# Moving eight of 128 key columns per half tile from VectorE to TensorE in a decode attention kernel

## The chip, the cores and the metric

The kernel runs on one core of a Trainium2 chip. The metric is device time in microseconds (us); lower is better. The profile is one execution taken by the hardware profiler, and its span is a little shorter than the time of a run (657.3 against 658.6 us in the profiled execution of the kernel before).

## The reference, cut to what matters

A decode step for two sequences: normalize `x`, one query for each of 32 heads, attention over a cache of 8192 keys and values a head, output projection, residual, and a small gated FFN.

```python
B, Sq, D = 2, 1, 512
Hq, Hkv, Sk, Dh = 32, 32, 8192, 128
...
scores = jnp.einsum("bhqd,bhkd->bhqk", q, k) * (Dh ** -0.5)
p = _softmax(scores, axis=-1)
o = jnp.einsum("bhqk,bhkd->bhqd", p, v)
```

K and V in bf16 are 2 x 32 x 8192 x 128 x 2 bytes = 134.2 MB each. With the weights the kernel reads 281 MB, each byte once.

## The kernel before: what the argument touches

The 64 pairs of sequence and head are taken in tiles of four (one `o` each), 16 tiles in all: 15 passes of a loop and a tail. A tile of K or of V is 8.39 MB and holds two half tiles, on each partition 128 columns (keys) of 128 values. There is **one buffer for K and one for V**, so a load can be issued only when the last reader of the tile before is done.

The scores of a half tile are shared out. VectorE takes the first `JC` columns: one multiply by q, four adds that halve the width, one reduce. TensorE takes the last `NG` groups of 8: it transposes them, ScalarE copies the transposes out of PSUM, TensorE multiplies them by q.

```python
GT = 8
NG = 4
JC = J - NG * GT          # J = 128 columns, so 96 are VectorE's
...
def k_mult(p, pr):        # VectorE
    return nc.vector.tensor_tensor(
        out=pr[:, 0:JC, :], in0=tile(K, p)[:, 0:JC, :],
        in1=q_c[:, Q2:QW].unsqueeze(1).broadcast_to([128, JC, Dh]), op=ALU.mult)
...
for g in range(NG):       # TensorE, for each half tile
    if g >= 2:
        wait(a2p, ev[g - 2])             # ScalarE has emptied this PSUM bank
    for k in range(GT // 2):
        ... nc.tensor.transpose(Tp[g % 2][...], k_t[:, j:j + 2, :] ...)
    if g >= 1:
        score(g - 1)
score(NG - 1)
```

SyncE issues the loads, all on one queue: K of the next tile when both multiplies (`d2s`) and the transposes (`kf`) are done, V when the last PV matmul is done.

```python
sp.wait((d2s, 2 * o - 1), tokp("kf", p))
if o < NI:
    load(K, A_k_cache, o, k_sem[0])
    sp.wait(tokp("pv", p))
    load(V, A_v_cache, o, v_sem)
```

The softmax here doesn't subtract the row's maximum and nothing guards it: scores larger than these inputs give would overflow.

## Time and profile before

| | before |
|---|---|
| time, median of 3 runs | 658.75 us (658.38 to 660.93) |
| busy: VectorE, TensorE, ScalarE | 467.8, 337.1, 271.2 us |
| DMA queue in use | 99.2% of the span |
| one pass of the loop | 38.70 us |
| V issued ahead of K's landing | 4.3 us |
| K issued ahead of V's landing | 6.1 us |

The last two rows: each is the time that a load, once issued, stands in the queue behind the load before it. I call it the **lead** of that load. While a lead lasts, a tile is still under way. One wait list, SyncE's own in the kernel before (columns: who waited for whom, total us, times, longest):

```profile
SPq L182 <- PE O L418: 303.0, 15, 20.8
SPq L32 <- PE S L378: 236.2, 15, 29.0
SPq L182 <- DVEq L602: 36.3, 15, 3.4
```

V (first line) waits for TensorE's PV matmuls. For K, SyncE waits for the transposes and then, 2.4 us a pass, for VectorE's multiplies: VectorE released K.

### The profile page before, as it was taken

The numbers are of one execution on the slowest core, as the hardware profiler recorded it, in microseconds if no ns is written. First come the engines' busy times: TensorE is split into PE (matmuls) and PEld (weight loads), VectorE is DVE, ScalarE is ACT, GpSimd is POOL, SyncE is SP. The second block draws the span as 40 slices with busy tenths as digits, with TensorE's granted clock in tenths as the row PEclk, the third lists the DMA queues.
The fourth block names the chain that finished last, engine by engine and source line by source line (L and its number), as shares of the span: only waits on it lengthen the run. The fifth ranks groups of instructions, "written<-read, shape, count | busy, mean of one in ns | idle before, by whom it ended". The sixth has DMA issues, their size and how long they took to land.

```text
span 657.3 us, 7744 instructions
## 1 busy us (share of the span) xinstructions
PE 337.1 (51%) x3097; PEld 207.1 (32%) x3097; DVE 467.8 (71%) x275; ACT 271.2 (41%) x687; POOL 95.3 (15%) x96
## 2 busy tenths in 40 slices
PE   2563644646354464534547364454736445473676
PEld 0250431515133151413316141231604224150444
DVE  1188594967949496794949769494985949589881
ACT  1352452625345172524527243352624336262460
POOL 4000011030300203030030303003030210303000
PEclk9955656555565655756565575656556565655566
DMA  9999999999999999999999999999999999999997
GB/s 415 403 428 440 431 423 431 439 439 423 423 447 439 419 427 439 447 439 415 435 435 447 431 419 427 447 447 427 415 435 447 439 431 415 439 447 410 427 421 312
DMA packets 6324, 281.16 MB, mean 428 GB/s; under 512 B 710, under 2 KB 812, under 8 KB 1324
## 3 DMA queue, kind: packets, MB, share of 16 engines
q1 hardware_dynamic: 6308, 281.05, 99.2%
q8 instruction: 5, 0.08, 0.0%
q14 instruction: 3, 0.02, 0.0%
q10 hardware_dynamic: 8, 0.00, 0.0%
HBM read 281.05 MB, written 0.00 MB: 428 GB/s over the span
## 4 chain that ended last, share of the span: by engine, by line
DMA 65%; DVE 32%; PE 2%; issue 1%; ACT 0%; SPq 0%; DVEq 0%; ACTq 0%
DMA K<-in_A_k_cache_dram 59%; DVE X L552 15%; DVE prod L552 15%; DMA K<-in_B_W_down_dram 5%; DVE prod L561 1%; DVE X L561 1%; PE T L395 0%; PE O L418 0%; DVE scores L566 0%; PE Ob L431 0%; ACT e L506 0%; PE O L816 0%; ACT kT L578 0%; SPq L708 0%; PE S L378 0%
## 5 line engine op out<-in xcount | busy, mean ns | idle before, releaser
L418 PE MATMUL O<-V,e 128*16 128x512 bf16 x1024 | 114.7, 612 | 187.6 <-ACT e L506 113.0
L552 DVE TENSOR_TENSOR X<-K,q_c 128x12288 bf16<-128x12288 bf16 x15 | 98.4, 6558 | 141.8 <-DMA K<-in_A_k_cache_dram 141.8
L578 ACT ACTIVATE kT<-T 128x1024 bf16<-128x1024 bf16 x128 | 126.9, 1022 | 151.9 <-PE T L395 148.6
L395 PE MATMUL T<-ident_f,K 128*128 128x128 f32 x512 | 126.0, 410 | 65.3 <-DVEq L598 60.8
L506 ACT ACTIVATE e<-scores 32x96 bf16<-32x96 f32 x128 | 52.9, 414 | 182.1 <-DVEq L609 178.4
L561 DVE TENSOR_TENSOR prod<-prod 128x6144 bf16<-128x6144 bf16 (+1 forms) x68 | 112.7, 1658 | 4.0
L552 DVE TENSOR_TENSOR prod<-K,q_c 128x12288 bf16<-128x12288 bf16 x17 | 111.4, 6553 | 2.9 <-DMA K<-in_A_k_cache_dram 2.1
L395 PEld LDWEIGHTS T<-ident_f,K 128*128 128x128 f32 x512 | 91.5, 211 | 67.4 <-DVEq L598 62.8
L418 PEld LDWEIGHTS O<-V,e 128*16 128x16 bf16 x1024 | 28.6, 117 | 260.6 <-ACT e L506 140.6
L561 DVE TENSOR_TENSOR X<-X 128x6144 bf16<-128x6144 bf16 (+3 forms) x60 | 99.5, 1658 | 3.8
L378 PE MATMUL S<-q_c,kT 128*128 128x8 bf16 x1024 | 48.7, 171 | 35.1 <-ACT kT L578 34.9
L533 POOL MEMSET O_l<- 128x32 bf16 x13 | 1.7, 131 | 422.0 <-DVEq L615 422.0
L378 PEld LDWEIGHTS S<-q_c,kT 128*128 128x128 bf16 x1024 | 42.0, 107 | 63.5 <-ACT kT L578 61.7
L538 POOL COPY rsel<-rows 128x112 bf16<-128x112 bf16 x14 | 44.1, 3151 | 41.2 <-DVEq L615 40.4
L431 PE MATMUL Ob<-sel,os_sb 128*128 128x4 f32 x136 | 30.9, 350 | 11.0 <-ACT os_sb L581 11.0
L431 PEld LDWEIGHTS Ob<-sel,os_sb 128*128 128x128 f32 x136 | 29.4, 319 | 12.9 <-ACT os_sb L581 12.8
L506 ACT ACTIVATE e<-S 32x32 bf16<-32x32 f32 x128 | 29.7, 232 | 2.4 <-PE S L378 0.9
L506 ACT ACTIVATION_READ_ACCUMULATOR e<-scores 32x1 f32 x128 | 29.1, 227 | 0.0
L506 ACT ACTIVATION_READ_ACCUMULATOR e<-S 32x1 f32 x128 | 25.6, 200 | 1.5
L540 POOL TENSOR_TENSOR O_l<-O_cur,mask 128x32 bf16<-128x32 bf16 x14 | 25.0, 1785 | 0.0
L549 POOL COPY q_c<-q_all 128x144 bf16<-128x144 bf16 x16 | 16.2, 1010 | 45.3 <-PE O L418 32.3
L578 ACT ACT_TABLE_LOAD x15 | 19.2, 1283 | 0.3
(106 smaller groups left out, 142.2 us busy)
## 6 DMA issues: line engine op xcount, KB each, us to landing
K<-in_A_k_cache_dram SPq DMA_DIRECT2D x2, 4096.0 KB, 20.8
V<-in_A_wq_dram SPq DMA_DIRECT2D x1, 4096.0 KB, 12.3
V<-in_A_v_cache_dram SPq DMA_DIRECT2D x1, 4096.0 KB, 22.8
X<-in_A_wo_dram SPq DMA_DIRECT2D x1, 3584.0 KB, 16.4
V<-in_A_v_cache_dram SPq DMA_DIRECT2D x1, 3072.0 KB, 29.7
K<-in_B_W_up_dram SPq DMA_DIRECT2D x1, 1376.0 KB, 28.8
K<-in_B_W_gate_dram SPq DMA_DIRECT2D x1, 1376.0 KB, 32.4
V<-in_A_v_cache_dram SPq DMA_DIRECT2D x1, 1024.0 KB, 31.7
```

Source lines behind the costliest of these rows:

```text
L378: i = nc.tensor.matmul(Sp[p % 2][:, A * jj:A * jj + 2 * A], lhsT=kv_[:, k, r, :], rhs=q_c[:, 2 * A * r:2 * A * r + 2 * A], start=(r == 0), ...
L395: i = nc.tensor.transpose(Tp[g % 2][:, k * 128:(k + 1) * 128], k_t[:, j:j + 2, :].rearrange("p j d -> p (j d)").bitcast(F32), ident_f[:])
L418: i = nc.tensor.matmul(Op[0][c:c + 16, :], lhsT=e_t[q][:, j // VJ, :], rhs=v_t[:, j:j + VJ, :].rearrange("p j d -> p (j d)"), start=(q == ...
L431: i = nc.tensor.matmul(Ob[:, 0:A], lhsT=os_sb[:, jj * Dh:(jj + 1) * Dh], rhs=sel[:, A * jj:A * jj + A], start=(jj == 0), stop=(jj == VJ - 1))
L506: i = nc.scalar.activation(out=e_t[q][h, j0 // VJ:j1 // VJ, :].rearrange("p g (j a) -> p g j a", a=A)[:, :, :, a], in_=src(h, a), func=ACT ...
L533: pool.run(e.memset(o_window(o - 1)[0], 0.0))
L538: e.tensor_copy(out=rsel[:, :, o % B, :], in_=bass.AP(x.tensor, x.offset, [list(x.ap[0]), [DR - OS, A], [1, DR]]))
L540: e.tensor_tensor(out=w, in0=O_cur[:].unsqueeze(2).broadcast_to([128, A, NM]), in1=mask[:, off // 4:off // 4 + OS // 4 * (A - 1) + 1:OS // ...
L549: nc.gpsimd.tensor_copy(out=q_c[:], in_=q_all[:, o]).then_inc(g2d, 1)
L552: return nc.vector.tensor_tensor(out=pr[:, 0:JC, :], in0=tile(K, p)[:, 0:JC, :], in1=q_c[:, Q2:QW].unsqueeze(1).broadcast_to([128, JC, Dh] ...
L561: run(nc.vector.tensor_tensor(out=pr[:, 0:JC, 0:w], in0=pr[:, 0:JC, 0:w], in1=pr[:, 0:JC, w:2 * w], op=ALU.add))
L578: to_pe(nc.scalar.activation(out=kT[gg % 2][:], in_=Tp[gg % 2][:].bitcast(BF16), func=ACT.Copy))
```

## The change

The intent: VectorE is the busiest compute engine and its multiplies stand in the chain that ended last, so give eight of its 96 columns to TensorE. One number changes; the rest of the diff follows from it, as ScalarE's counter reaches other values.

```diff
-    NG = 4
+    NG = 5
...
-                EV = 13
+                EV = 15
...
-                    k_part(body, 0, (1, 2, 3, 4), ((k2p, 1),))
-                    k_part(body, 1, (5, 6, 7, 8), ())
-                    collect(body, 9)
-                    pv(body, 0, ((JC, J, ((v_sem, 16), (a2p, 10))), (0, JC, ((a2p, 12),))))
+                    k_part(body, 0, range(1, 6), ((k2p, 1),))
+                    k_part(body, 1, range(6, 11), ())
+                    collect(body, 11)
+                    pv(body, 0, ((JC, J, ((v_sem, 16), (a2p, 12))), (0, JC, ((a2p, 14),))))
...   (the tail's counts likewise)
```

More of the change, by code (lines that the diff above doesn't have):

```diff
@@ L469, in program @@
                 t_ob_loop = (pe.sem, tail.at["ob"])
-                k_part(tail, P0, (2, 3, 4, 5), ((k2p, 1),))
-                k_part(tail, P1, (7, 8, 9, 10), ((k2p, 2),))
-                nc.tensor.wait_ge(a2p, 12)
+                k_part(tail, P0, range(2, 7), ((k2p, 1),))
+                k_part(tail, P1, range(8, 13), ((k2p, 2),))
+                nc.tensor.wait_ge(a2p, 14)
                 nc.tensor.wait_ge(sem_wo, 16)
@@ L478, in program @@
                 tail.mark("op", i)
-                pv(tail, P0, ((JC, J, ((v_sem, 16),)), (0, JC, ((a2p, 13),))))
-                nc.tensor.wait_ge(a2p, 14)
+                pv(tail, P0, ((JC, J, ((v_sem, 16),)), (0, JC, ((a2p, 15),))))
+                nc.tensor.wait_ge(a2p, 16)
                 for c in range(DC):
@@ L484, in program @@
                         start=False, stop=False, skip_group_check=True)
-                pv(tail, P1, ((V_LAST, J, ((sem_vl[0], 16), (a2p, 15))), (0, V_LAST, ((a2p, 15), (sem_vl[1], 16)))),
+                pv(tail, P1, ((V_LAST, J, ((sem_vl[0], 16), (a2p, 17))), (0, V_LAST, ((a2p, 17), (sem_vl[1], 16)))),
                    lambda: tail.mark("z", z_sum(Sp[0])))
@@ L722, in program @@
                 sums()
-                collect(tail, 16)
+                collect(tail, 18)
                 dve.wait(tok("ob", NI))
```

## The prediction

> **What bounds the kernel now.** I began with the page's header, slices and queues.
>
> ```profile
> PE 337.1 (51%) x3097; PEld 207.1 (32%) x3097; DVE 467.8 (71%) x275; ACT 271.2 (41%) x687; POOL 95.3 (15%) x96
> ...
> DMA  9999999999999999999999999999999999999997
> ...
> q1 hardware_dynamic: 6308, 281.05, 99.2%
> ```
>
> No compute engine is above 71% of the span, while the 16 DMA engines are nine tenths busy or more in every slice but the last, and one queue's packets fill 99.2% of their time. The kernel reads a cache once: 281.05 MB at the page's 428 GB/s is 656.7 us, the whole span of 657.3 us. The change alters no byte.
>
> The chain that ended last looks less simple: DMA 65%, DVE 32%, with the two multiplies of line 552 (K times q, 96 columns each) at 15% each. In order of time, one loop pass reads:
>
> ```profile
> 422.46 6.56 DVE X L552
> 429.02 6.48 DVE prod L552
> 435.58 25.46 DMA K<-in_A_k_cache_dram
> 461.03 0.04 DVEq L598
> ```
>
> So K lands, VectorE multiplies its two half tiles for 13.1 us, the buffer is free, the next K is issued and lands 25.46 us later: a loop of 38.7 us. The reader is to ask whether those 25.46 us are transfer or queueing. SyncE's timeline gives the issue times, and TensorE's shows when V landed:
>
> ```profile
> 417.97 0.33 SPq L182 DMA_DIRECT2D V<-in_A_v_cache_dram  x1
> 435.58 0.33 SPq L182 DMA_DIRECT2D K<-in_A_k_cache_dram  x1
> 456.69 0.33 SPq L182 DMA_DIRECT2D V<-in_A_v_cache_dram  x1
> ...
> 441.72 1.03 PE L418 MATMUL O<-V,e 128*16 128x512 bf16 x8 [4.50 <-DMA V<-in_A_v_cache_dram]
> ```
>
> V, issued at 417.97, landed at about 441.7; K, issued at 435.58, had **6.1 us** to stand in the queue behind it. K's remaining 461.03 - 441.7 = 19.3 us are its transfer: 8.39 MB in 19.3 us is 434 GB/s. The next V was issued at 456.69, **4.3 us** before K landed at 461.03. There is thus always a tile under way when the next is issued. A pass moves 16.78 MB, and 16.78 MB / 38.70 us = 433.5 GB/s, the same rate. The busy time by stretches confirms it (columns: stretch, length, then busy time of PE, PEld, DVE, ACT, POOL, the clock, DMA share, GB/s):
>
> ```profile
> 447.00:452.00 5.00, 1.81 (x20) 0.32 (x12) 4.86 (x5) 0.00 (x0) 3.64 (x3) 0.83 1.00 433
> 452.00:456.70 4.70, 2.79 (x25) 0.84 (x25) 0.06 (x1) 2.94 (x9) 0.00 (x0) 0.52 1.00 432
> 461.10:499.80 38.70, 20.14 (x174) 12.51 (x174) 28.72 (x15) 16.53 (x42) 6.21 (x5) 0.50 1.00 434
> ```
>
> The rate is 433 where VectorE is busy, 432 where it rests and 434 over a pass. The VectorE part of the chain is therefore not the limit: its 13.1 us run while V streams, and shortening them lengthens the wait in the queue by as much.
>
> [...]the trace's slope, (6553 - 3358) ns / 6144 elements = 0.52 ns[...]. So fewer columns do save VectorE time in proportion.
>
> **The change part by part.** Per half tile, eight of 128 columns move from VectorE to TensorE, with ScalarE evacuating the transposes.
>
> *VectorE loses* 1024 elements in the multiply (0.53 us at 0.52 ns), 512 + 256 + 128 + 64 in the four adds (0.50 us) and 64 inputs in the reduce (0.07 us, from 953 ns for 768 inputs[...]): 1.1 us a half tile, 2.2 a pass, about 35 us in all: busy 468 to 433.
>
> *TensorE gains* one group a half tile: 4 transposes (128 more in all, 410 ns each, 52 us of busy at most) and 8 score matmuls (256 more, 171 ns: 44 us at most by the mean, partly pipelined). What counts is the time that it adds to the stretch: transposes of successive groups start at 424.89 and 426.04, so 1.15 us a group, 2.3 us a pass.
>
> *ScalarE gains* one evacuation a half tile: 32 times 1022 ns = 33 us in all (271 to 304), inside those 1.15 us. The Exp instructions trade 8 columns between the two kinds, 32 against 96 columns at 232 and 414 ns, so the sum is unchanged.
>
> Now the two releases that feed the queue. **K's buffer** needs both multiplies and the transposes. Counted from the start at 422.43, the multiplies now end at +13.1 and the transposes at +10.7 (first score matmul of the last but one group of the second half, 433.14). Afterwards: multiplies +13.1 - 1.07 = +12.0, transposes +10.7 + 2.3 = +13.0. The wait changes hands from VectorE to TensorE, and K is issued at about +13.1, within 0.2 us of before. It could be 6 us later before the queue ran dry. **V's buffer** is free after the last PV matmul, which waits for the Exp of VectorE's last scores. Those come 2.2 us earlier. TensorE's and ScalarE's longer first part ends in time: the Exp of TensorE's scores ended at 438.84 and would end near 441.3, still ahead of V's landing at 441.7 and of VectorE's first scores at about 442.2. The last stretch also has 22 matmuls in place of 24 (2.74 us to 2.5). So V is issued some 2.4 us earlier, near 454.3, and stands about 6.7 us in the queue where it stood 4.3. Both margins stay positive, and a pass stays at 38.7 us.
>
> At the ends: the first K lands at 35 us, after 13 MB that nothing here touches. In the tail, the FFN weights are issued near 619 and land at up to 654.13, behind V, so an issue one or two us earlier or later is queueing as well. The last Exp ended at 640.6, before V's last parts released TensorE at 641.6 and 644.2; VectorE there gets 1 to 2 us shorter. The last matmuls wait for the FFN weights as before. Sum over the span: 0 us, within a few tenths.
>
> **The rivals.** *The chain taken at its word*: 30% of 657 us in the multiplies, 8% shorter, gives 16 us, 642 us. For it speaks only that view; against it, the bytes: 642 us would need 438 GB/s on average with the slow ends included, more than any pass moves. *TensorE and ScalarE become the bound*: the K part grows by 2.3 us and ScalarE's evacuations are serial. If each group cost twice my 1.15 us, K would be issued at +15.3, 2.2 us later and still 3.9 us before the queue ran dry. Only at about four times my estimate would time be lost; no row suggests it. *A lower granted clock*: the mean is 0.574 and the K part already runs at 0.50 in the stretches that I looked at[...]. *DMA slowed or eased by other traffic*: 433 against 432 GB/s above speaks against an effect over a fraction of a per cent. It would be a few us at most.
>
> **Range and chances.** Centre: 658.5 us, the fastest two of three runs before (658.38, 658.75). The third was 660.93, so a median could fall there by chance. Range 657.0 to 660.5 us: 1.5 us below for slightly better filling of the queue, 2 above for scatter of that size. Two per cent is 13 us; downward it would need bytes to be saved, upward an error in a margin of several us in each pass: faster 0.01, same 0.97, slower 0.02.
>
> **What would show it.** DMA still at nines and about 434 GB/s a pass; K issued every 38.7 us; VectorE's busy time near 433 us, ScalarE's near 304, and 128 more transposes; SyncE's last wait before K naming TensorE in place of VectorE; K's landing about 25.4 us after its issue; V issued about 6.7 us before K lands. In the chain, the multiplies would be replaced by transposes and evacuations with no gain. The prediction is wrong if a pass shows stretches where DMA has nothing under way, or if the rate with more TensorE traffic leaves 434 GB/s by over 1%.

What no trace or run of this case shows is cut, and the cuts are marked. No term of the sum is among them: it came to 0 us, within a few tenths. That the rate of a pass cannot rise rests on the rates by stretches alone (433, 432 and 434 GB/s); that 434 is a ceiling was not shown. The 0.52 ns is the trace's: VectorE's multiply of 12288 elements took 6553 ns and its first add, of 6144, 3358 ns. The reduce's 0.07 us used an estimate; measured, the reduce took 953 ns for 768 inputs and, after the change, 886 ns for 704, 0.07 us less. "Partly pipelined" is to be read from TensorE's timeline: eight score matmuls took 0.38 us together (at 424.66), where eight times 171 ns would be 1.37. Of the clock only this was measured: 0.50 in the K part before (422.4 to 435.5) and after (422.1 to 436.6), and a mean of 0.574 in the trace before and 0.599 in that after; that it could not fall further was not shown.

## The result, and the profile after

657.47 us, median of 6 runs (657.32 to 657.57), against 658.99 us for 6 runs of the kernel before (658.38 to 660.93). The ratio is **0.9971**, 95% interval 0.9957 to 0.9985. A ratio here is the mean time of one kernel's fast runs over that of the other's of the same rounds, so it is not quite the ratio of the two medians. The change is the same within 2%, a gain of 0.3%. The scatter shrank too: 0.25 us between the extremes against 2.55.

The page of the changed kernel, the lines that answer to those of before:

```profile
PE 371.9 (57%) x3480; PEld 236.3 (36%) x3481; DVE 432.7 (66%) x275; ACT 304.6 (46%) x719; POOL 88.7 (14%) x96
...
DMA  9999999999999999999999999999999999999997
...
q1 hardware_dynamic: 6308, 281.05, 99.3%
...
DMA 64%; PE 22%; ACT 7%; DVE 6%; issue 1%; DVEq 0%; SPq 0%
```

VectorE's busy time fell by 35.1 us (467.8 to 432.7) and the time by 1.5. The DMA line is unchanged. In the chain VectorE's 32% became 6%, and TensorE and ScalarE took its place with 29%: the chain was rewritten, and the end hardly moved. One pass of that chain, in order of time (start, us, what), with its first and last link, shows what happened:

```profile
422.11 1.13 PE T L395 x4
...
435.46 0.05 PE S L378
...
435.57 25.15 DMA K<-in_A_k_cache_dram
460.72 0.04 DVEq L598
```

K is now released by TensorE's transposes and first scores, 13.5 us after the pass began, where VectorE's multiplies released it after 13.1. K landed 25.15 us after its issue, where it was 25.46. The two add up to the same 38.7 us. SyncE's waits say it as well; the line that named VectorE is gone:

```profile
SPq L32 <- PE S L378: 305.2, 15, 31.2
SPq L182 <- PE O L418: 268.5, 15, 18.9
```

And SyncE's timeline shows the one thing that did move in the loop:

```profile
435.57 0.33 SPq L182 DMA_DIRECT2D K<-in_A_k_cache_dram  x1
454.08 0.33 SPq L182 DMA_DIRECT2D V<-in_A_v_cache_dram  x1
```

V is issued at 454.08, so 460.72 - 454.08 = **6.6 us** before K lands, where the lead was 4.3.

Where did the 0.3% come from, then? Passes that start from the first multiply can be compared one by one. The second pass of the kernel before, and the third (columns: stretch, length, busy time of PE, PEld, DVE, ACT, POOL, clock, DMA share, GB/s):

```profile
73.74:112.84 39.10, 20.13 (x175) 12.49 (x175) 28.71 (x15) 16.53 (x42) 6.22 (x3) 0.54 0.99 429
112.84:151.54 38.70, 20.13 (x175) 12.48 (x175) 28.71 (x15) 16.52 (x42) 6.21 (x5) 0.50 1.00 434
```

and of the changed kernel:

```profile
73.83:112.54 38.71, 22.77 (x199) 14.46 (x199) 26.51 (x16) 18.59 (x44) 5.75 (x3) 0.54 1.00 433
112.54:151.23 38.69, 22.72 (x199) 14.50 (x199) 26.52 (x15) 18.61 (x44) 5.75 (x5) 0.54 1.00 434
```

The engines did the same work in both passes of the kernel before, yet the second took 0.4 us longer, with the DMA at 0.99 and 429 GB/s. After the change the second pass is like the third. So the kernel before lost some DMA time, with VectorE not the cause within that pass. That led to the theory that I tested, the **queue theory**: a lead of 4.3 us was not quite enough, some of the 16 DMA engines ran out of work before V's load reached them, and the change helped by issuing V 2.3 us sooner. The rivals: VectorE's shorter work was itself on the path; TensorE's work or clock was the cause; or the gain was made after the loop alone (the **end theory**).

### The profile page after: what moved, and what is told of

It reads as the page before. It is cut to its first block, busy times and chain, and to the rows that moved or that the text cites. A ratio compares the mean times of both kernels' runs of the same rounds, so it can differ in the third digit from the quotient of the medians.

```text
span 656.1 us, 8543 instructions
## 1 busy us (share of the span) xinstructions
PE 371.9 (57%) x3480; PEld 236.3 (36%) x3481; DVE 432.7 (66%) x275; ACT 304.6 (46%) x719; POOL 88.7 (14%) x96
## 2 busy tenths in 40 slices
DMA packets 6324, 281.16 MB, mean 429 GB/s; under 512 B 710, under 2 KB 812, under 8 KB 1324
## 3 DMA queue, kind: packets, MB, share of 16 engines
q1 hardware_dynamic: 6308, 281.05, 99.3%
## 4 chain that ended last, share of the span: by engine, by line
DMA 64%; PE 22%; ACT 7%; DVE 6%; issue 1%; DVEq 0%; SPq 0%
DMA K<-in_A_k_cache_dram 59%; PE T L395 16%; ACT kT L578 7%; DMA K<-in_B_W_gate_dram 5%; PE S L378 5%; DVE prod L552 2%; DVE prod L561 2%; DVE X L561 1%; DVE X L552 1%; DVE scores L566 0%; PE O L816 0%; PE O L764 0%; DVEq L617 0%; DVEq L598 0%; DVE kT L824 0%
## 5 line engine op out<-in xcount | busy, mean ns | idle before, releaser
L578 ACT ACTIVATE kT<-T 128x1024 bf16<-128x1024 bf16 x160 | 160.0, 1022 | 196.5 <-PE T L395 192.7
L395 PE MATMUL T<-ident_f,K 128*128 128x128 f32 x640 | 161.7, 416 | 100.7 <-DVEq L598 94.8
L552 DVE TENSOR_TENSOR X<-K,q_c 128x11264 bf16<-128x11264 bf16 x15 | 90.4, 6026 | 172.5 <-DMA K<-in_A_k_cache_dram 172.5
L395 PEld LDWEIGHTS T<-ident_f,K 128*128 128x128 f32 x640 | 114.5, 213 | 102.8 <-DVEq L598 96.8
L561 DVE TENSOR_TENSOR prod<-prod 128x5632 bf16<-128x5632 bf16 (+1 forms) x68 | 104.3, 1533 | 4.0
L552 DVE TENSOR_TENSOR prod<-K,q_c 128x11264 bf16<-128x11264 bf16 x17 | 102.3, 6020 | 6.2 <-DMA K<-in_A_k_cache_dram 4.5
L506 ACT ACTIVATE e<-scores 32x88 bf16<-32x88 f32 x128 | 51.1, 399 | 105.4 <-DVEq L609 103.9
L561 DVE TENSOR_TENSOR X<-X 128x5632 bf16<-128x5632 bf16 (+3 forms) x60 | 92.0, 1533 | 3.7
L378 PE MATMUL S<-q_c,kT 128*128 128x8 bf16 x1280 | 60.8, 171 | 40.1 <-ACT kT L578 40.0
L538 POOL COPY rsel<-rows 128x112 bf16<-128x112 bf16 x14 | 40.4, 2885 | 39.5 <-DVEq L615 38.7
L506 ACT ACTIVATE e<-S 32x40 bf16<-32x40 f32 x128 | 31.9, 249 | 2.4 <-PE S L378 0.9
```

The costliest lines, as they stand in the source:

```text
L378: i = nc.tensor.matmul(Sp[p % 2][:, A * jj:A * jj + 2 * A], lhsT=kv_[:, k, r, :], rhs=q_c[:, 2 * A * r:2 * A * r + 2 * A], start=(r == 0), ...
L395: i = nc.tensor.transpose(Tp[g % 2][:, k * 128:(k + 1) * 128], k_t[:, j:j + 2, :].rearrange("p j d -> p (j d)").bitcast(F32), ident_f[:])
L506: i = nc.scalar.activation(out=e_t[q][h, j0 // VJ:j1 // VJ, :].rearrange("p g (j a) -> p g j a", a=A)[:, :, :, a], in_=src(h, a), func=ACT ...
L538: e.tensor_copy(out=rsel[:, :, o % B, :], in_=bass.AP(x.tensor, x.offset, [list(x.ap[0]), [DR - OS, A], [1, DR]]))
L552: return nc.vector.tensor_tensor(out=pr[:, 0:JC, :], in0=tile(K, p)[:, 0:JC, :], in1=q_c[:, Q2:QW].unsqueeze(1).broadcast_to([128, JC, Dh] ...
L561: run(nc.vector.tensor_tensor(out=pr[:, 0:JC, 0:w], in0=pr[:, 0:JC, 0:w], in1=pr[:, 0:JC, w:2 * w], op=ALU.add))
```

## The experiments

Twelve kernels ran, in three sets; each set shares its runs of the kernel before (medians 659.67, 660.21 and 659.84 us; 11 runs each). The record names a different chip for each set, so ratios, which are taken within a set, are compared here, and medians of different sets only roughly. All outputs passed the comparison with the reference. That includes three that were wrong on purpose, so this comparison does not notice a few per cent of missing keys, or stale ones, and their passing is no sign that they are right.

### The kernel before against itself

No edit.

> The kernel before against itself, for the noise: ratio 1.000 within 0.002, and scatter of 1 to 2 us among its runs as in the six seen (658.38 to 660.93). Queue theory (a V issued only 4.3 us before K lands lets some DMA engines run dry now and then): single passes longer than 38.70 us, as the second pass of the first trace (39.1). End theory (the gain of the change is made after the loop): passes all alike, and the last FFN weights let TensorE go near 654.2.

Measured: 659.64 us (659.03 to 662.12), ratio 0.9996 (0.9970 to 1.0022). In its trace the second pass took 39.28 us, so the long second pass is no accident of one trace. But the time after the loop was longer too (below), which the end theory had not expected of it.

### VectorE's part alone

```diff
     JC = J - NG * GT            # NG = 4, as before
+    JV = JC - 8                 # VectorE's multiply, adds and reduce, and ScalarE's Exp of them, use JV
```

> VectorE on 88 columns, TensorE still on 32; columns 88 to 95 get no scores, so the result is wrong on purpose. VectorE's pass is 2.2 us shorter, TensorE's as before. Queue theory: V issued near 454.3, about 6.6 us before K lands, so all of the change's 0.3% is here, 657.5 us. Theory that VectorE's time in the chain is on the path: 15 passes times 1.1 us, about 642 us. End theory: also near 657.5, with the FFN weights issued 1 to 2 us earlier.

Measured: 657.68 us (657.17 to 658.67), ratio 0.9962 (0.9939 to 0.9986). Within the noise all of the gain is here, with TensorE as before. It is not 642 us, so VectorE's time in the chain was not on the path, as predicted. V was issued at 454.00, 6.7 us before K landed, and the second pass took 38.70 us.

### TensorE's part alone

```diff
     JC = J - NG * GT            # NG = 5, as after
+    JV = JC + 8                 # VectorE still works on 96 columns
```

> TensorE transposes and scores 40 columns, VectorE still works on 96 (8 of them twice, its results for these unused); the result is right. Queue theory: V is issued at about 456.7 as before, 4.3 us before K lands, so no gain: 658.9 us and scatter like before. Theory that the clock or TensorE's traffic made the gain: 657.5. Theory that K's later release costs: K issued at +13.4 instead of +13.1 us, slower by 0.3 us a pass, 663 us; the queue theory says 0 of this.

Measured: 659.13 us (658.04 to 660.11), ratio 0.9983 (0.9959 to 1.0007): unclear, as its interval holds both 1 and the changed kernel's 0.9971. The lead was 4.5 us and the second pass 39.16 us, as in the kernel before. The later release of K cost nothing. This run speaks for the queue theory by its pass, not by its time.

### The changed kernel with V issued later

In each pass ScalarE makes some idle copies after its last Exp, and V's load waits for them too. The work of the other engines is untouched. First try, two copies:

```diff
+                    for r in range(2):
+                        nc.scalar.activation(out=idle[:], in_=wo_last[:], func=ACT.Copy).then_inc(vi, 1)
+                        nc.scalar.wait_ge(vi, r + 1)
+                    nc.scalar.sem_inc(vx, 1)
+                    nc.scalar.sem_inc(vi, -2)
...
-                            sp.wait(tokp("pv", p))
+                            sp.wait(tokp("pv", p), (vx, o))
```

> The changed kernel with two idle ScalarE copies of about 1.9 us each after the last Exp of a pass, and V's load waiting for them: V issued some 2 to 3 us later, back to about 4.3 us before K lands; nothing else moves within the loop. Queue theory: the gain goes, 658.9 us with scatter. End theory, and any theory that puts the gain in VectorE's or TensorE's work: still 657.5 us.

Measured: 658.07 us (657.81 to 658.46), ratio 0.9967 (0.9945 to 0.9990). The dose was too small: the two copies took 3.85 us, 1.93 each, but began at 451.32, during the PV matmuls, so V was issued only 1.2 us later, at 455.29, with a lead of 5.5 us. Most of the gain is still there, so the idle copies themselves are not what costs: this run is the control for the next. Three copies of 1792 elements put it right:

> The changed kernel with three idle ScalarE copies, about 5.1 us in all, so that V is issued near 456.4, as in the kernel before (4.3 us before K lands; the earlier try with two moved it by 1.2 us alone, and ended at 658.1). Queue theory: 658.5 to 660 us, scatter of 1 us or more, a pass or two over 38.7 us. End theory: 657.5 to 658 us.

Measured: 661.01 us (659.41 to 663.32), ratio 1.0011 (0.9986 to 1.0036). This interval and the changed kernel's (0.9957 to 0.9985) just do not overlap. **The gain is gone and the scatter is back**, 3.9 us between the extremes, though VectorE, TensorE and their order are those of the changed kernel. The lead was 461.56 - 457.40 = 4.2 us. V's issue and the end of K's landing in one pass, then the second and third pass:

```profile
457.40 0.33 SPq L184 DMA_DIRECT2D V<-in_A_v_cache_dram  x1
...
461.56 0.04 DVEq L600
```

```profile
73.70:113.20 39.50, 19.97 (x199) 13.46 (x199) 26.52 (x16) 23.50 (x47) 5.75 (x3) 0.63 0.99 428
113.20:151.91 38.71, 22.03 (x199) 13.83 (x199) 26.52 (x16) 23.42 (x47) 5.75 (x5) 0.59 1.00 432
```

VectorE is busy for 26.52 us in both, as after the change, and the long second pass is back at 39.50. Six copies then took the lead away altogether:

> Six idle copies of 1.93 us: V issued near 463, some 2 us after K has landed, so that the queue is empty in each pass (the first transposes' evacuation of the next pass is held up by about 3 us too, which K's margin of nearly 6 us should swallow). Queue theory: each of 15 passes longer by 2 us of emptiness[...], 710 to 725 us. If V's issue did not matter: 657.5 us.

Measured: 695.34 us (694.89 to 695.87), ratio 1.0528. Right in kind, too high by 15 to 30 us in my figure. V was not late in each pass: it was issued in turn after K's landing (by some 2.2 us at 76.04, for a landing just before 73.87, and by less than 1 us later on) and up to 1 us before it (at 116.19 for one just before 117.21), and the 13 passes that follow the first took 41.3 us on average, 2.6 us more each. My figure was 657.5 us and 15 passes times some 4 us, 717.5 in the middle. Half of the 4 us was a term for the time to the first bytes, which no run had measured; without it the same sum is 687.5 us. The first packets of these loads are on record 0.7 to 1 us after the issue (between 158.84 and 159.09 for 158.09). V's lead is not all that the copies changed: they run into the next pass, and in every other pass K too was issued later (16.0 us into the second pass, 13.4 us into the third).

### The transfers taken away

Both kernels with the loop's loads after the first tile's cut to 8 of the 256 columns of a tile (a 32nd; the expectation says a 16th by mistake):

```diff
-                            load(K, A_k_cache, o, k_sem[0])
+                            load(K, A_k_cache, o, k_sem[0], 0, 8)
                             sp.wait(tokp("pv", p))
-                            load(V, A_v_cache, o, v_sem)
+                            load(V, A_v_cache, o, v_sem, 0, 8)
```

> The kernel before with the loop's loads of K and V cut to 1/16 of their columns for 14 of the tiles (wrong result on purpose): compute alone sets the pass. VectorE then runs without a pause, 28.7 us a pass in place of 38.7: about 659 - 14 x 10 = 520 us.

> The changed kernel with the same cut. If the change saves VectorE 2.2 us a pass and transfers alone hide it: 26.5 us a pass, some 31 us under few_before, about 487 us. If TensorE and ScalarE took over as the bound: little or nothing under few_before.

Measured: 542.13 us (541.23 to 543.19) and 523.54 us (522.52 to 524.70). The change is worth 18.6 us, 3.4%, where transfers do not hide it, a clear gain but not the 31 us that I expected. One pass of each, from VectorE's first multiply to the next, first before, then after:

```profile
248.88:279.41 30.53, 17.20 (x174) 10.07 (x174) 28.71 (x15) 16.41 (x42) 6.21 (x5) 0.61 0.06 17
```

```profile
240.60:269.41 28.81, 18.69 (x198) 10.75 (x198) 26.51 (x16) 18.36 (x45) 5.75 (x5) 0.68 0.06 18
```

VectorE works 2.2 us less, exactly as worked out. But I had left its pauses out: 1.8 us in the first line, and 2.3 to 2.7 in the later passes after the change, which took 28.8 or 29.2 us in turn (a few earlier ones took up to 30.2; passes 3 to 14 took 29.15 us on average). The waits name the new one; the line has no counterpart of that length before:

```profile
DVE scores L566 <- PE Ob L431: 13.1, 14, 1.9
```

VectorE's reduce now waits for TensorE's collect matmuls, which come after the longer K part. Part of the saving turns into a wait for TensorE as soon as it is exposed.

### More lead for V, with nothing else changed

V's two halves are loaded separately, the first as soon as the first half tile's PV is done:

```diff
-                            sp.wait(tokp("pv", p))
-                            load(V, A_v_cache, o, v_sem)
+                            sp.wait(tokp("pv", p - 1))
+                            load(V, A_v_cache, o, v_sem, 0, J)
+                            sp.wait(tokp("pv", p))
+                            load(V, A_v_cache, o, v_sem, J, 2 * J)
```

> The kernel before, every engine's work unchanged; V is loaded as two halves, the first issued when the first half tile's PV is done (about 448, 13 us before K lands), the second when the whole is done, as before. Queue theory: no engine runs dry, so all of the change's gain comes without the change: 657.5 us, ratio 0.996 to 0.998, scatter under 1 us. Theory that the gain lies in VectorE's or TensorE's work: 659 to 661 us.

> The changed kernel with V loaded in two halves likewise. Queue theory: a lead of 6.7 us was already enough, so nothing is left to win, 657.5 us. If the lead still mattered: under 657.

Measured: 659.02 us (658.93 to 660.19), ratio 0.9990 (0.9975 to 1.0005), and 659.14 us (658.97 to 659.40), ratio 0.9988 (0.9974 to 1.0002). My 657.5 us was wrong for both. What the theory says of the pass came true, but at a price that I had not counted. Passes two and three of the kernel before with split loads:

```profile
73.94:112.73 38.79, 20.08 (x175) 12.51 (x175) 28.70 (x16) 16.51 (x42) 6.21 (x3) 0.54 1.00 433
112.73:151.50 38.77, 20.14 (x175) 12.53 (x175) 28.71 (x16) 16.52 (x42) 6.21 (x5) 0.54 1.00 433
```

The long second pass is gone with VectorE still at 28.7 us of work, and four of the five runs lie within 0.31 us. But every pass takes 38.78 us in place of 38.70: 15 passes make 1.2 us, about what the filled queue gains. The page counts 8484 packets in place of 6324; that the greater number is the cause of the slower pass fits, and was not tested. So splitting V is no better kernel, and for the changed kernel it is a loss against 657.5.

### Further along the same road

```diff
-    NG = 5
+    NG = 6          # and 8, with ScalarE's counts to match
```

> TensorE takes 48 columns, VectorE 80. VectorE's pass is 2.2 us shorter once more; K is released by TensorE's transposes 2.4 us later, at about +15.9 us, some 3.4 us before V lands. Queue theory: V's lead is ample, K's is now the short one, so dry moments come back: 658.5 to 662 us with scatter. Theory that VectorE's time is on the path: under 657.

> TensorE takes 64 columns, VectorE 64. K would be released at about +20.7 us, 1.5 us after V has landed, so the queue is empty once a pass: 2 to 4 us a pass for emptiness and the time to the first bytes, 685 to 715 us. If TensorE's part stayed hidden: 657.5 us.

Measured: 670.38 us (667.48 to 674.13), ratio 1.0156, and 710.21 us (708.23 to 713.27), ratio 1.0765. With 48 columns on TensorE, VectorE's busy time fell again, to 397.4 us, and the kernel is 10.5 us slower than before. K was issued 15.8 us into a pass (448.85 for a pass that began at 433.01), and TensorE started on V at 452.70, so the lead was under 4 us; the passes took 39.5 us on average. I had expected 658.5 to 662, so a lead of under 4 us for K seems to cost far more than one of 4.3 us for V. That is argued, not shown: TensorE and ScalarE work more in this kernel too. Two passes in which the clock rose (a mean of 0.72 in the first of them, from 472.55, against 0.54 in the pass from 114.87) and K was issued 13.7 and 14.1 us after their start took 38.69 us, which fits; the pass after them, with K at 15.8 us again, took 38.75, which does not. With 64 columns the queue runs empty before K is issued (at 477.31, where the DMA share is 0.01 or less in each us from 475 to 478), and the page's DMA line shows it:

```profile
DMA  9988979999898999979899898999989899999996
```

The time to the first bytes, which the expectation for 64 columns counts, was 0.7 to 1 us with V late, above, and 1.0 us at the start of the kernel before, where SyncE's first load was issued at 0.81 and its first packets are on record at 1.82.

Of 32, 40, 48 and 64 columns, 40 is the best, and the room is narrow: fewer on TensorE shorten V's lead, more shorten K's.

### The traces side by side

Loop passes run from the first multiply of one to that of the next. The last column but one is the time from the start of the last loop pass to the end of the span.

| kernel | V's lead, us | second pass | passes 3 to 14, mean | last pass to end | time, median |
|---|---|---|---|---|---|
| before | 4.3 | 39.10 | 38.70 | 80.0 | 658.99 |
| before, again | 4.4 | 39.28 | 38.71 | 80.9 | 659.64 |
| TensorE's part alone | 4.5 | 39.16 | 38.70 | 80.2 | 659.13 |
| after, V as late as before | 4.2 | 39.50 | 38.72 | 80.7 | 661.01 |
| after, V 1.2 us later | 5.5 | 38.70 | 38.70 | 79.3 | 658.07 |
| after | 6.6 | 38.71 | 38.70 | 79.1 | 657.47 |
| VectorE's part alone | 6.7 | 38.70 | 38.70 | 79.6 | 657.68 |
| before, V split | 13.2 | 38.79 | 38.78 | 79.3 | 659.02 |
| after, V split | about 15 | 38.77 | 38.78 | 79.2 | 659.14 |

All four traces with a lead under 5 us have a second pass over 39 us and at least 80.0 us at the end; all five with 5.5 us or more have neither. Some 0.4 to 0.8 us of the gain is thus in the second pass and 0.4 to 1.7 us, mostly about 1, after the loop's last pass began. That the second pass follows V's lead is shown, by one trace of each kernel; the slower runs of the scatter were not traced. For the end it is likely, not shown: 79.6 and 80.0 us lie close together, and the end also varies by itself. In the kernel before, TensorE waited 0.86 us for the gate weights; in its second trace it did not wait there, but V's last part let it go later.

The granted clock does not sort the kernels: VectorE's part alone has the gain at 0.565 to 0.593, where the kernel before had 0.564 to 0.579 in the same set, and the changed kernel with V late has lost it at 0.595 to 0.615, where the changed kernel had 0.589 to 0.625. What did go with it is TensorE's speed: four transposes took 1.09 us where it was 0.50 in the changed kernel (424.58), and 0.64 us where it was 1.00 in the same kernel with its transfers cut (275.96).

One more view of these traces bears on why it is the second pass that suffers. Before it, the packets of the 16 DMA engines are on record nearly together, so the GB/s of half-us stretches come in bursts: from 50 to 73 us their standard deviation is 1.1 to 1.6 times their mean in the first seven traces of the table. From 80 to 110 us it is 0.43 to 0.76 of the mean in the four with a lead under 5 us, and still 1.07 to 1.33 in the other three. With the short lead the engines thus fall out of step in the second pass, as they would if some of them ran out of work before others. That reason is my inference, not shown: which of them waited, and why the passes that follow lose nothing, stays open.

## Why the prediction was right, point by point

**The bound** held: DMA at nines, 99.3% of the queue, 434 GB/s a pass and 38.7 us a pass, with VectorE's work 35 us shorter. VectorE's part alone left the time at 657.68, and the rival that took the chain at its word (642 us) fell.

**The sizes of the parts**: VectorE 432.7 us for 433 predicted, ScalarE 304.6 for 304, V issued at 454.08 for 454.3 with a lead of 6.6 us for 6.7. K was issued at +13.5 us in place of +13.1, within 0.4 rather than 0.2, because TensorE's +13.0 took the start of the first score matmul for the release: that matmul started at +13.2 (435.27), and the step from there to the issue is 0.3 us. It was queueing all the same. In some passes the clock rose and K came up to 0.7 us sooner after the last, as at 396.27 after 358.18, 38.1 us later (clock 0.75 from 389.4 to 396.3, against 0.50 from 422.1 to 436.6). The passes did not follow.

**The sum** was the term that was off: "0 us, within a few tenths" was -1.5 us. The step behind it is "There is thus always a tile under way when the next is issued". As read from whole tiles it is true, and the range had 1.5 us below its centre for "slightly better filling of the queue". But 4.3 us of lead did not fill all of the queue all of the time; issuing V as late again brought the loss back with every other part of the change in place. The small distance from the centre is in part luck: 658.5 us came from the two fastest of three runs and lies 0.5 us under the median of all six, 658.99.

**That TensorE and ScalarE stay hidden** held for eight columns. With 16 it fails. The prediction's "Only at about four times my estimate would time be lost" took a lead of nearly nothing as the limit, K issued some 6 us later than before. With 48 columns K was issued 2.7 us later than before (15.8 us against 13.1), and the kernel was already 10 us slower. If K's short lead is the cause, as argued above, this is the same mistake as in the sum, a lead above zero taken for enough.

**That fewer columns save VectorE time in proportion** held for its busy time, 2.2 us a pass: the multiply went from 6553 to 6020 ns for 11264 elements in place of 12288, again 0.52 ns an element. With the transfers cut, some 1.4 us a pass of it showed in the time (30.53 against 29.15 us), the rest became waits.

## What to carry to other kernels

Where a busy engine stands in the chain that ended last, ask whether the DMA in that chain was moving bytes or queueing: take the landing of the load before it from the total, and compare the rate. Here passes moved 434 GB/s, with the DMA share at 1.00, and 2.2 us a pass taken from VectorE came back as queueing: a pass stayed at 38.70 us. What was still gained was lead, the time by which each load is issued before the one ahead of it lands. With these 8.39 MB loads on one queue, the kernels with a lead of 4.2 to 4.5 us for V took some 1 to 3 us of 658 longer than the changed one (ratios 0.9983 to 1.0011 against 0.9971), and the one with 5.5 us hardly longer (0.9967). So balance the work between engines by the leads that you measure, and not so that the busy times are equal.
